# The fifth head pair's keys and queries through the DMA crossbar, more buffers, and a new order of all engines, in a fused attention and gated-convolution kernel

## The chip, the cores and the metric

One core of one Trainium2 chip. The time is device microseconds of one execution of the whole program, as the median of plain runs; one further execution is recorded by the hardware profiler, and all views of the profile are of that one.

## What is computed

Two layers in a row, on a batch of 4 and a sequence of 768. The first is block-sparse attention with 8 heads of 64: blocks of 32 tokens, each of which sees itself and its neighbours, the first and the last block, and three sampled ones.

```python
scores = scale * np.matmul(q, k.transpose(0, 1, 3, 2))        # 4 x 8 x 768 x 768
mask = (np.abs(blk_i - blk_j) <= 1) | (blk_i == 0) | (blk_j == 0) | (blk_i == 23) | (blk_j == 23)
mask |= sampled blocks
attn = softmax(np.where(mask, scores, -1e9))
x = np.matmul(attn, v)                                        # heads side by side: 4 x 768 x 512
h = np.maximum(x @ w_in, 0.0)                                 # 512 -> 1024
conv_out[:, s] = conv_w[0] * h[:, s-1] + conv_w[1] * h[:, s] + conv_w[2] * h[:, s+1]
out = (h * sigmoid(conv_out)) @ w_out                         # 1024 -> 512
```

Inputs and output are float32; the kernel multiplies in bfloat16.

## The kernel before

**Pairs, slots, units.** The 32 heads (4 batches of 8) are taken as 16 pairs P = 0 to 15, four to a batch. A pair's transposed keys and queries lie in two tiles of one of five slots, `e` for even and `o` for odd columns of 128 (64 feature rows, and 24 mask rows below them that add -8000 to forbidden scores). The scores are computed for all 768 keys of a head, half of the queries at a time (a segment: a batch and a half, the last half cut in two, 9 in all). The work is cut into 144 units of 8 blocks of 128 x 128: two groups of score matmuls into a PSUM tile `st` (L746), one exp of 128 x 1024 on ScalarE into `pt` (L757), and two groups of value matmuls into `av` (L779). Pair P of the first batch is first used at unit 4.5 P; pair 4, the fifth, at unit 36, pair 5 at 40.5, pair 6 at 45, pair 7 at 49.5, pair 8 at 72.

**After the attention.** Per segment and pair VectorE normalises `av` into `xtok` (L698), which is transposed to `xT`, for most by a crossbar DMA on SyncE's queue (L707), for a few on TensorE (L717). Then come the first matmul with `winb` into `mix` (L895), ReLU into `hE` (L915 on ScalarE or L917 on VectorE), the convolution as three products and two sums on VectorE (L949, L959; in the last segment as matmuls with diagonal matrices, L970), tanh on ScalarE (L998) and the gate into `gT` (L1001, L1006), the second matmul with `woutb` (L825, the last token tile L810), a copy to `o2s` (L328 on ScalarE, L330 on VectorE; these two lines are the copies of every kind) and the store (L833).

**Keys and queries reach their slots in two ways.** `kq_transposes(P)`, used for P < `NPE` = 5, loads keys (192 KB) and the first query half (96 KB) into `nat`, transposes them on TensorE (6 transposes at L470, 4 at L508) into PSUM and copies them to the slot on VectorE or ScalarE; the second query half goes later through a buffer `nq` (4 more transposes). `kq_crossbar(P)`, used for the rest, loads keys and (up to batch 2) whole queries into `nat`, sends each through the crossbar DMA, keys first, into a staging tile `stg` on SyncE's queue, and then copies both halves on VectorE:

```python
for x, l in ((1, [lk]), (0, lq)):
    xb.append(op("xb", {"SP": 1.4}, lambda e, x=x: nc.sync.dma_start_transpose(          # L585
        out=stg_t[sg.index][:, x].rearrange("p h c s -> p (h c) s"), in_=nat_t[nb.index][:, x]), ...))
for x, t in enumerate((E_t, O_t)):
    def cp(e, x=x, t=t):
        dcopy(e, t[slot.index][0:64], stg_t[sg.index][64 * x:64 * x + 64])                # L330
```

Both copies depend on both crossbars. Loads of keys, queries, values and weights are issued by GpSimd (L240), which also converts to bfloat16. From the second query halves on, they follow the list `SEQ`, and each waits, by a one-element copy on GpSimd (`pace`, L660), until the load four places before it has landed; from the third batch on, a `pace` (L417) reads the result of a set exp instead. The mask rows of slots 3 and 4 are copied by four DMAs on SyncE's queue (L361).

**What sets the order.** There is no run-time scheduler. The operations are collected in a list, and `put_down` issues them in an order written out by hand in the string `ORDER`: two characters name an operation, one more its engine if it may run on several (A is ScalarE, V VectorE, S SyncE), then one for each buffer it takes. Each engine works off its share strictly in that order, and each queue too, so a waiting instruction holds back all behind it on its engine. `NFILL` filler matmuls stand early on TensorE, where it has little else to do.

```python
def put_down(ops, order):
    ...
            o = ops[64 * CODE.index(line[x]) + CODE.index(line[x + 1])]
            if len(engines) > 1:
                e = ENGINES[line[x]]
            for b in o.allocs:
                b.index = CODE.index(line[x])
            ...
                o.fn(e)
```

Of the kernel before, what the change touches and what calls it, by code (L numbers as in the profile page):

```python
# [25 lines left out]
5L5p5q5u0N0J1aV5811bV1S00O0P0Q0R461A0470S481O1490T4a1U14b1V4c2414d2604e274f2c24g2e2591TV34h2f4i2k04j2m34k5H2
5M35v5P05Q5R41pV1oV5z4O15A05U15V5I4PV00I5B25C5J5N5O5W5610625a05S5T5X5Y630661675bV5Z05+5D15EV641656b06c5/060V
6811B11DV1CV6g16h6d26i3ht0hu6l0hq1hrhsV0hvAhO06m6t1hz06u6n46v5hw1hxhAhyAhPhQhBVhRhW16y06z696a6A06D16EhS6F1hT
hF06e1P1hG6fhYhHV6I06j6JhX6k6o6Q16R6q11QV6p06whI06xhJ1RVhZhUh+6r6K26S3hKA6V06WhL16+16/hM6X4705h/0w6s125V4hV0
hC0hDhNVhEVia26B6C6G730747816H6L6M6T1796U6Y1W16Z1Z07507a1i23ib6N21XV46O280296P1/A7g07h7i27l17m717276777n37b7c0  # L30
7q07r7s47j7k7v17w7o7pi0i4i31+Vi51YV7d0i6i1ic7e7x57D07E7t7F07uio07y7z7I17J7N0ii17G17Oijip7Hi77K12g12h7f7A1id7B
i8iei92aV07P27C2bVif7L7S17Tiq7M7Q7R7X07Yik7U37Z42n4l2s14m2u2002v1ig2dV0ih0k2lV1831847Vil88089ir8558a08d18e7W7+
7/0868i08j2iV12tV2imV02jVisV18020K818f18k2iu1iv8q18rix0iyiwA2o02pizViS0iUiT2qV22rViV8s38v08w8x487iD18A18B8C5
iA0iB8F0iE8b8c8G8g8K18h8L2x2w2C2y1822iCAiFA8H02F2G02D28M1i+1iWiXiM0iN8l8S08m2118TiOVi/8U2iP08X18t18Y8u8y8z8D
8Z322Vj0j18n023V8oiQiRA9008E8I8J91iG195196iHiJ0iK8N924975j2iYje3iZj3iIVjf8P1iLV8Qj629d09e8O08V8W8+9i19j9f08/93
9498999n09o9g19hj8j4j79a2j9j5ja9bjhjgji9k19p39s19tjs19x09y9u59z09l9m9qjE09F19r9G9v9K09LjFjb2I2H2Q2N2R22T2O09H2
8p2z2J08R2K9cjjjt9w9A9B09I9J9P19Qjcjdjkjl2AV39M1jujG9R49U09V9N9W3jva019Oa1jHjwA2a50a69Sa25jK19TjL9X9Y2LV42EV3
2MVjIV32BV9C09Da70aa1jN0abjOjMA1a31af0jT1agjUac2jPVk60jVV0Mk8k70Gk9ak1ala4jQ0ah4am32/2S3032Y2Z13231373829E0in
2U0itjJ2Va8jRas0atjSAjW1ax1aya9au1jXjZ0adj+az5jYAj/A2PV4kake19Z19+9/km2knkokpkfkqkbkckhaC0aDaeaiaH1aE0k31aIaj
kgkd1ank4k5Aap2jy0jzaP0aQk01ao0jAavawaAaBaJ2aR4aU1jBaVaZ0k1a+aFkrjCA0aW3a/1aGaKaLjm0b21b3jnb45kik2VaM0ku3aNkj  # L40
kvkwkxb70job8aS0bf1aTaXjpaYkI1bgb90bk0b0b1b5jqA1kkaqklkskyjx33134aOarbh2ktkzkC0kJblkDbm4bp1kKb6bqbabu0bvbb1
2+V02WV02XVkAkBkE35V1bc13a3b13f3cbr3bw1kLkFbibC1bDbH0bIbd39V1kGV336VkMA2kO1kR0kPkSbE5bJ0kTAbM1bNbjbR0bSbnbobs
btkU0bO2bxbykVbW1bXkQVla0lclbbT4kWAbY3bz0ldbAlelfkX1bF0kYc20bGbKbLkZVli1c3c71c8bPl10k+1l2c453d3e3m3p3q03u3n03r
3s3tlglkljl3Vllc91cc0cdce0bQk/ch1cibUl70bVbZcp0b+1l8cqc5l0Vlmcj2lnl41cu1cvcr4cw3c6cal5cz0cAcbcfcgckcE1cFclcB5
cG1be1kHjr3g03hlq2b/2lrlslolhltc0lul9Vcm1l6Vlpcnly3lzlAlBlvlClwlxcs0ctcxcJ0lM0cKlG1cycR1cScClNcDcHcL2cT4cW0cX
cY33E3B3F23J3G3H3C13I3Q3R2lHcIcMcN1c/1d0cUcVcZd40d5lOc+lIlD3v1bBc1cod10d65dc1ddde1cO0lElF3oV2cPlPd2lJdh0di0H
lKV33iV23jVlQA1dj2d3dm1dnm20d7do4m51d8m6dr0m33wd923xV3m4V0m7Adsdw1dxmq0mrdamtms3DV3dt3dy03T3U33Y3V3W3X43440me1
df0dgmh0dkmfmidE0dFdJ1mgAmjAm81dKm9mb0mcdG5maAdL1mu3yVmdVmy1mG2mvmHmAmwmzmBdO0dldpdqdudvdzdPdB1dT1mn1mk0mldA1
dUdHdQ2lRkNlL3K0cQ23L3Z1jD3+dbmmAdV4d/0modImpAlS0e0e13mCmO33MV4mImQdCmJlTe41e5lUlVe60mDmEmKmx0mFlY1lWA13SA4lZ
e90eaeb5l+ee1efdMdNdRdSdWdXe20dY0mPdZe3n00e7ej0e8mLeg1ekl/n1er1m0A2mR45V0mMmS0LmN3/V0el23ldDd+413AmTmUmV3NVec  # L50
edehmW1eiesmXew0exmYn2et4ey3eB1eCeD0mZn3emeG0eHeO1en1ePn4V340Veo2epm+A0nc1nf0ndngeI5eQ1nhAneVnC0nDnEnFnGeT0eU
eueY1evn61eZezeAn7eV2f10f2e+4f33nHn8Vn90eEeFnanbVnu1eJeKf61f7fe0ffeR0eSnl1nmeWnwnveL1nnVnxf80fg5fj1fkfl1eXni0
fo0fpfq2lX3k423O3Peq03ze/njno1ft1f0f4f5fuf9fB0fCnpnInynznkVnJnK2eMnLnr0fa1nsfhfinAfb0nMfcnqVnBnNfv4fD3fG1fHfm
fL0fnfMfrfsfwfxfE0fFntAfI0fy2nOfznS3nTnUnVnWfN5fT1fUfV1o40fJfY0fZn+1o5g11g2fKn/fOfPfW1fXnPf+2g34nXeNm/fdn5fAnQ
nRf/g0g90gag4ge1gfg5gb3o0o6nYnZgg0gj0o7fQ1o8V1g60fRo1gkgr1gsom0ono2A0g7ooV1op1oqgl5orAgc0gdoK0oMgt1os0ghgigw0
gxgmgnotov1owgB1gCgu1go2gpoLoNoOgy2ouAoxAgD4fS1oS1gqg8oH0gK0oIgLoB1oCgvgzgAgEoJAoE0gP1gQgM3oPoFgFgR0oToDVoUoV
# [57 lines left out]
def kernel(  # L114
# [23 lines left out]
    NF, NPE = 4, 5  # L138
# [79 lines left out]
    NFILL = 21  # L218
# [851 lines left out]
```

## Time and profile before

| | |
|---|---|
| plain runs | 206.13 us median of 3 (206.09 to 208.36) |
| the profiled execution | 207.49 us, span on the core 205.7 us |
| TensorE, ScalarE, VectorE, GpSimd busy | 197.3, 190.3, 180.3, 57.9 us |
| DMA moved | 25.96 MB, 126 GB/s on average |
| first and last exp start | 6.72 and 186.60 us |

Busy time of an engine counts the recorded length of each instruction; neighbours overlap in their ends, so an engine at 96% still has some room, and the share says little of a single stage. In the views below a line is given as start, length, engine, line of the code and operation; PE is TensorE, PEld its weight loads, ACT ScalarE, DVE VectorE, POOL GpSimd, SP SyncE, and a q behind the name is the engine's issuing of DMAs. In brackets stands how long the engine was idle ahead of the instruction and what ended it.

### The profile page before, as it was taken

To read this page: it belongs to the slowest core of one execution; us is meant where nothing else is said; L and a number is where in the kernel's file an instruction comes from. 1 tells how busy PE (TensorE), PEld (TensorE's weight loads), DVE (VectorE), ACT (ScalarE), POOL (GpSimd) and SP (SyncE) were. 2 spreads that over 40 slices of the span, in tenths; PEclk is the share of its full clock that TensorE was granted. 3 is DMA by queue.
4 is the path that set the end of the run, shared out by engine and by line. 5 is a ranking of instruction groups with operands and counts; after the bars stand their busy time and mean duration, and the time that the engine had idled before them with its cause. 6 is when DMAs were issued, how large, how long until landed. Compare 5 with 4: busy or idle time off the path is not lost.

```text
span 205.7 us, 6845 instructions
## 1 busy us (share of the span) xinstructions
PE 197.3 (96%) x2698; PEld 154.4 (75%) x2716; DVE 180.3 (88%) x570; ACT 190.3 (93%) x252; POOL 57.9 (28%) x112
## 2 busy tenths in 40 slices
PE   7999999999999999999999999998999999999992
PEld 7789978886688877776788877766688877785761
DVE  6978969997899997999899989979799978999950
ACT  6999999998999999999899999998999999997852
POOL 8870468630514226102415386100000000000000
PEclk9999999999999999999999999999999999999999
DMA  6999999999798983999997999993210401310523
GB/s 147 173 208 208 185 138 117 147 151 189 97 150 96 156 116 35 208 201 192 93 186 88 119 134 225 118 208 72 75 28 3 146 17 29 115 51 17 202 76 133
DMA packets 53655, 25.96 MB, mean 126 GB/s; under 512 B 39616, under 2 KB 50584, under 8 KB 53624
## 3 DMA queue, kind: packets, MB, share of 16 engines
q0 software_dynamic: 19984, 11.24, 45.9%
q1 hardware_dynamic: 33064, 13.60, 34.3%
q10 hardware_dynamic: 576, 0.69, 0.9%
q8 instruction: 21, 0.34, 0.7%
q14 instruction: 10, 0.08, 0.2%
HBM read 23.08 MB, written 6.29 MB: 143 GB/s over the span
## 4 chain that ended last, share of the span: by engine, by line
PE 57%; ACT 16%; DMA 11%; DVE 10%; issue 3%; POOL 0%; ACTq 0%; DVEq 0%
PE st L746 18%; PE mix L895 14%; PE mix L825 13%; ACT pt L757 12%; PE av L779 10%; DMA stg<-nat 6%; DMA nat<-in_k_dram 3%; DVE m L949 3%; DVE m L959 2%; DVE hE L917 2%; DMA o2s<-in_q_dram 1%; PE mix L810 1%; ACT o L328 1%; ACT m L998 1%; DVE xtok L698 1%
## 5 line engine op out<-in xcount | busy, mean ns | idle before, releaser
L757 ACT ACTIVATE pt<-st 128x1024 bf16<-128x1024 f32 x144 | 140.0, 1034 | 2.8 <-PE st L746 2.1
L779 PEld LDWEIGHTS <-pt 128*128 128x128 bf16 x1152 | 51.8, 97 | 9.8
L779 PE MATMUL av<-vt,pt 128*128 128x65 bf16 x1152 | 59.1, 193 | 0.1
L895 PE MATMUL mix<-xT,winb 128*128 128x384 bf16 (+2 forms) x288 | 55.0, 308 | 0.5 <-DVE o2s L330 0.2
L949 DVE TENSOR_SCALAR m<-hE,cw 128x382 bf16<-128x382 bf16 (+2 forms) x192 | 49.0, 314 | 0.6 <-ACT hE L915 0.3
L825 PE MATMUL mix<-woutb,gT 128*128 128x512 bf16 x159 | 43.9, 379 | 1.3 <-DVE gT L1006 0.7
L746 PE MATMUL st<-o 88*128 88x128 bf16 (+1 forms) x240 | 44.4, 229 | 0.2
L746 PE MATMUL st<-o,e 88*128 88x128 bf16 (+1 forms) x228 | 43.4, 233 | 0.4 <-DVE o L330 0.3
L746 PE MATMUL st<-e 88*128 88x128 bf16 (+1 forms) x208 | 41.6, 239 | 0.8 <-ACT pt L757 0.2
L746 PE MATMUL st<-e,o 88*128 88x128 bf16 (+1 forms) x224 | 42.2, 234 | 0.1
L746 PEld LDWEIGHTS <-e 88*128 88x128 bf16 x436 | 33.5, 97 | 10.4 <-issue 1.7
L746 PEld LDWEIGHTS <-o 88*128 88x128 bf16 x464 | 34.9, 97 | 7.8 <-issue 0.9
L959 DVE TENSOR_TENSOR m<-m 128x764 bf16<-128x764 bf16 (+2 forms) x64 | 34.0, 532 | 0.3
L895 PEld LDWEIGHTS <-winb 128*128 128x128 bf16 x288 | 23.2, 97 | 6.6 <-issue 1.1
L998 ACT ACTIVATE m<-m 128x764 bf16<-128x764 bf16 (+2 forms) x32 | 26.4, 826 | 0.2 <-DVE m L959 0.2
L825 PEld LDWEIGHTS <-gT 128*128 128x128 bf16 x184 | 15.7, 97 | 9.6 <-DVE gT L1006 0.8
L417 POOL COPY pace<-pt 1x1 bf16<-1x1 bf16 x24 | 6.4, 267 | 51.3 <-ACT pt L757 51.2
L917 DVE TENSOR_SCALAR hE<-mix 128x384 bf16<-128x384 f32 x28 | 15.4, 554 | 4.0 <-PE mix L895 3.6
L915 ACT ACTIVATE hE<-mix 128x384 bf16<-128x384 f32 (+2 forms) x36 | 17.5, 505 | 1.2 <-PE mix L895 1.0
L1006 DVE TENSOR_TENSOR gT<-m,hE 128x764 bf16<-128x764 bf16 (+3 forms) x36 | 18.1, 510 | 0.4
L698 DVE TENSOR_TENSOR xtok<-av,rcp 128x384 bf16<-128x384 f32 (+2 forms) x36 | 18.1, 506 | 0.4
L240 POOL DMA_DIRECT2D nat<-in_q_dram x23 | 16.8, 733 | 2.7 <-issue 2.5
(84 smaller groups left out, 158.3 us busy)
## 6 DMA issues: line engine op xcount, KB each, us to landing
out_dram<-o2s SPq DMA_DIRECT2D x22, 256.0 KB
vn<-in_v_dram POOLq DMA_DIRECT2D x16, 192.0 KB, 5.5
nat<-in_k_dram POOLq DMA_DIRECT2D x15, 192.0 KB, 4.9
nat<-in_q_dram POOLq DMA_DIRECT2D x7, 192.0 KB, 5.1
winb<-in_moe_w_in_dram POOLq DMA_DIRECT2D x2, 512.0 KB, 9.2
woutb<-in_moe_w_out_dram POOLq DMA_DIRECT2D x4, 256.0 KB, 8.2
nat<-in_q_dram POOLq DMA_DIRECT2D x8, 96.0 KB, 4.6
nq<-in_q_dram POOLq DMA_DIRECT2D x5, 96.0 KB, 5.3
```

The lines of the kernel that those rows point to most:

```text
L698: nm = op("norm", {"DVE": t_dps(128 * C)}, lambda e: nc.vector.tensor_tensor(out=xtok_t[xk.index][:, 0:C].rearrange("p c h d -> p h c d"), ...
L746: nc.tensor.matmul(out=st[:, 128 * x:128 * (x + n_)], lhsT=QK[kc % 2][s][0:88, 1, hh, kc // 2, :], rhs=QK[par][s][0:88, 0, hh, idx:idx + n ...
L757: nc.scalar.activation(out=pt_t[ptb.index], in_=st_t[stb.index], func=AF.Exp, bias=0.0, scale=0.125)
L779: nc.tensor.matmul(out=o[:, off:off + 65], lhsT=pt_t[ptb.index][:, 128 * x:128 * x + 128], rhs=V_t[vslot_b[P].index][:, hh, kc, 0:65], sta ...
L825: nc.tensor.matmul(out=acc(), lhsT=gT_t[gb.index][:, ffc, 128 * t:128 * t + 128], rhs=woutb[:, ffc, :], start=(ffc == 0), stop=(ffc == NFF ...
L895: nc.tensor.matmul(out=mix_t[hb.index][:, w1 * y:w1 * y + w1], lhsT=winb[:, fc, 128 * ffc:128 * ffc + 128], rhs=xT_t[xt_buf[n].index][:, f ...
L915: i = nc.scalar.activation(out=dst, in_=src, func=AF.Relu, bias=0.0, scale=0.5)
L917: i = nc.vector.tensor_scalar(out=dst, in0=src, scalar1=0.5, scalar2=0.0, op0=ALU.mult, op1=ALU.max)
L949: i = nc.vector.tensor_scalar(out=m_t[cb.index][:, x, y, 0:w], in0=hE_t[heb.index][:, f0 + y, t0 + x:t0 + x + w], scalar1=cw[:, x, f0 + y: ...
L959: nc.vector.tensor_tensor(out=m[:, a_, :, 0:w], in0=m[:, a_, :, 0:w], in1=m[:, b_, :, 0:w], op=ALU.add)
L998: th = [op("tanh", {"ACT": t_act(2 * w) + 0.04}, lambda e, cb=cb, w=w: nc.scalar.activation(out=m_t[cb.index][:, 0, :, 0:w], in_=m_t[cb.in ...
L1006: i = nc.vector.tensor_tensor(out=gT_t[gtb.index][:, f0:f0 + 2, t0:t1], in0=m_t[cb.index][:, 0, :, 0:w], in1=hE_t[heb.index][:, f0:f0 + 2, ...
```

## The change

`NPE` falls from 5 to 4, so pair 4 is made by `kq_crossbar` instead of `kq_transposes`; its second query load (`nq4`) leaves `SEQ`, and its first becomes a load of both halves. Eight kinds of buffer get one or two more: staging tiles 2 to 3, `nat` 4 to 5, value loads `vn` 3 to 4, `pt` 6 to 8, `xtok` 3 to 4, `xT` 3 to 4, the gate's `m` 4 to 5, output `o2s` 4 to 5. Two filler matmuls go. `ORDER` is another string throughout; the operations are the same but for pair 4.

```diff
 ORDER = """
-000b1e0010x020y030407080a0905060c0e0gV0d0WV10hA0UA0oA0f0B0z0i0XV0mV0VV0lV0nV0t0v1f1c01q11s21t1801E21G31m11Hr41
...
+0a0407080905060y000b1e01f1c01q11s11t1E21G21801m10102030A1H1S30O0P0Q0R0c0e0gV0d0WV30UV0hA0oA0f0x0iqZ1q+q/r0r1r2
...
-    NF, NPE = 4, 5
+    NF, NPE = 4, 4
     WHOLE = ()
-    SEQ = "nq0 nq1 w0 w1 nq2 w2 nq3 w3 k4 q4 v4 k5 q5 v5 k6 q6 v6 k7 q7 v7 nq4"
+    SEQ = "nq0 nq1 w0 w1 nq2 w2 nq3 w3 k4 q4 v4 k5 q5 v5 k6 q6 v6 k7 q7 v7"
...
-    NSLOT, NSTG, NNAT, NVN, NPT, NXK, NXT, NHE, NCV, NGT, NOS = 5, 2, 4, 3, 6, 3, 3, 2, 4, 2, 4
+    NSLOT, NSTG, NNAT, NVN, NPT, NXK, NXT, NHE, NCV, NGT, NOS = 5, 3, 5, 4, 8, 4, 4, 2, 5, 2, 5
...
-    NFILL = 21
+    NFILL = 19
```

In the new order the engines' instructions differ so. ScalarE: 3 of the 28 ReLUs of 128 x 384 and one value copy go to VectorE, one output copy comes from there, and the head's small copies are dealt anew. TensorE: 14 transposes and 2 fillers fewer. SyncE's queue begins, after the first loads and the two mask copies of slot 3, with the crossbars of pair 4, the two mask copies of slot 4 and the crossbars of pair 5; the first feature transpose follows them, then pair 6, three feature transposes and pair 7. Before, the feature transpose came first, and they alternated. GpSimd's queue has the same loads in nearly the same order, without `nq4`.

More of the change, by code (lines that the diff above doesn't have):

```diff
@@ L26 @@
[L26 to L55, printed above, removed]
@@ new lines @@
+bjaVaWbf434313233513936kdaGkpkok61kqkekv1krksa+kB0kCaHakklkm2QV0kt2RV2/V1kua/bk1kwbn0bokxb3bv1bwbp6kDb40kykE
+bx3bA0bB2UV0b50kFV0b630VkzA3bF1bC5kK1bGkH0kIbH7kLbbbK0bLbP1kMAkJVl32l4l5l6l7bM0kQ0bcbQkN1kRkObgbhbX0bYbR2kSA
+c01blbmkPAlb4bZ4c1bqc21kW0kXbrc50by1bzbDc6bEca1cbl8lcld33V1bs2kYVbtlel9lfkT1bIbJbNkUbOc73373j3k2383g3h03o3l3m
+3n3vcc6lgkVVbSci0cjbT0bU1lab+kZ0ck5bVlj3cn1col01l1k+cp7lllhk/Vl2Acs0b/c3ctc4c8c9cx1cdcecylF1lklmcf3lr0lilnlslt
+cglulvcu0cz2cC0cDcE4cl1cmcqcrcK1cLcM1lojk3a1b70bukG3p0bW3b3qchlz0lAcP0cvcwcQcR3lGcU1cVcAcBcFcG0cNcOcScTcZ0c+lp
@@ L62 @@
+qYAqIqJqKqLA1qMA
 """
```

44 lines of the change are left out of this document (34 added, 10 removed).

## The prediction

> **What bounds the kernel now.** I read the busy shares first, then busy time by stage, then the timelines of ScalarE, VectorE and the two issuing queues around pairs 4 and 5, where the change is made.
>
> ```profile
> PE 197.3 (96%) x2698; PEld 154.4 (75%) x2716; DVE 180.3 (88%) x570; ACT 190.3 (93%) x252; POOL 57.9 (28%) x112
> ```
>
> Three engines are near full, so the span is close to work divided among them, and a wait costs only where all three run out of cover. The stages show where that is:
>
> ```profile
> core 0: us, PE busy (x) PEld busy (x) DVE busy (x) ACT busy (x) POOL busy (x), PEclk, DMA share, GB/s
> 6.70:20.00 13.30, 12.90 (x216) 11.60 (x217) 10.95 (x34) 13.18 (x17) 6.79 (x10) 1.00 1.29 201
> 31.00:44.00 13.00, 12.67 (x219) 10.81 (x217) 12.89 (x40) 12.93 (x17) 9.29 (x18) 1.00 1.12 141
> 44.00:60.00 16.00, 15.13 (x191) 11.23 (x193) 13.82 (x40) 14.96 (x19) 2.73 (x6) 1.00 1.37 149
> 60.00:75.00 15.00, 14.82 (x237) 12.11 (x237) 14.79 (x45) 15.00 (x18) 5.30 (x10) 1.00 0.92 121
> 187.60:205.70 18.10, 14.00 (x121) 8.90 (x121) 10.50 (x44) 9.50 (x23) 0.00 (x0) 0.99 0.32 117
> ```
>
> From 6.7 to 20 us ScalarE alone is full (13.18 of 13.30) while VectorE has 2.4 us free. From 31 to 44 VectorE and ScalarE are both full. From 44 to 60 none is: TensorE 0.9 short, ScalarE 1.0, VectorE 2.2, with the DMA share at its highest. The last 18 us are a chain with 4 us of TensorE idle. The clock is full nearly throughout, so it plays no part. The timelines say what was missing at 44 to 60 (first ScalarE, then VectorE):
>
> ```profile
> 10.66 17.72 ACT L757 ACTIVATE pt<-st 128x1024 bf16<-128x1024 f32 x19
> 50.61 4.76 ACT L757 ACTIVATE pt<-st 128x1024 bf16<-128x1024 f32 x5 [0.65 <-PE st L746]
> ```
>
> ```profile
> 49.05 0.55 DVE L330 COPY e<-stg 64x1536 bf16<-64x1536 bf16 x1 [1.21 <-DMA stg<-nat]
> 52.91 0.55 DVE L330 COPY e<-stg 64x1536 bf16<-64x1536 bf16 x1 [0.71 <-DMA stg<-nat]
> ```
>
> The copies out of the staging tile wait for the crossbar of pairs 5 and 6, and exp 40, the first of pair 5, starts 0.65 us late behind that. The third such wait (1.1 us, near 75) is on VectorE alone. Sync's queue and GpSimd's show why it landed late:
>
> ```profile
> 36.59 1.30 SPq L707 DMA_TRANSPOSE xT<-xtok  x1
> 37.99 3.15 SPq L585 DMA_TRANSPOSE stg<-nat  x2
> ```
>
> ```profile
> 26.57 0.72 POOL L240 DMA_DIRECT2D nat<-in_k_dram  x1
> 27.61 0.72 POOL L240 DMA_DIRECT2D nat<-in_q_dram  x1
> 31.07 0.72 POOL L240 DMA_DIRECT2D nat<-in_k_dram  x1 [0.20 <-issue]
> 32.09 0.76 POOL L240 DMA_DIRECT2D nat<-in_q_dram  x1
> ```
>
> Pair 5's loads are issued at 31.07 and 32.09, but its two crossbars only at 37.99 to 41.14: the feature transpose at 36.59 stands ahead of them in Sync's queue and waits for VectorE's normalisation. The data then take 49.05 - 41.14 = 7.9 us.
>
> **The change, part by part.** Durations are rows of this execution, which took 207.49 us: the 205.74 us span and 1.75 around it. The median of the plain runs is 206.13, so I work out a difference and take it from the median.
>
> ```profile
> L330 DVE COPY e<-stg 64x1536 bf16<-64x1536 bf16 x11 | 5.9, 548 | 3.0 <-DMA stg<-nat 3.0
> L470 PE MATMUL mix<-ident,nat 128*128 128x128 bf16 x27 | 2.3, 219 | 0.0
> q0 software_dynamic: 19984, 11.24, 45.9%
> q1 hardware_dynamic: 33064, 13.60, 34.3%
> ```
>
> *Pair 4 to the crossbar.* TensorE loses 6 key and 8 query transposes. Ten ran from 39.35 to 40.19 and four took 0.39 us at 61.34: 1.23 us at most; at the spacing inside those groups, (0.50 - 0.22) / 5 = 0.056, 14 are 0.78. VectorE loses copies of 0.50, 0.56, 0.41, 0.41 and 0.30 = 2.18 and gains two staging copies, 0.55 + 0.58 = 1.13; ScalarE loses one of 0.37. The bytes loaded stay the same (one query load of 192 KB for two of 96). New are two crossbars of 0.197 MB. The page gives that queue 34.3% of 205.7 us for 13.60 MB, 5.2 us of all 16 engines per MB, so 1.0 us each, 2.0 us in a stretch whose DMA share is 1.1 to 1.4.
>
> *When they land.* Key and query loads issue at 26.6 and 27.6 and take the page's median 4.9 and 5.1: there at 31.5 and 32.7. Sync's queue is empty then (in the new order these two stand ahead of the feature transposes, after only two mask copies); at 1.25 us an issue the second goes out by 34. With 5.0 us (the transpose at 132.04 on the chain of waits) to 7.9 us after that, they land between 39 and 42. In the new order the first staging copy stands between two old places on VectorE that fell at 40.0 and 43.0; by its work ahead, at about 41.5, or 40.7 with ScalarE's lead below. So from 1.7 early to 1.3 late: nearest to the row under the same load, 7.9, which is 1 late. I price this at 0.4 and keep -0 and +1.3. Queued behind that copy on VectorE are the normalisations and convolutions, hence the next feature transposes.
>
> *Pairs 5 and 6.* Their crossbars no longer stand behind the feature transpose at 36.59 and can issue when their loads are there, about 37 to 39: 2 us earlier. The third staging buffer lets pair 6 follow without waiting for pair 5's copies. That removes up to 1.21 + 0.71 of VectorE's waits and the 0.65 + 0.33 of ScalarE's. Behind it stand two crossbars more on the DMA engines, 2.0 us. I take 0.6 off, bounds 0 and 1.9. The mask copies for slot 4, moved behind pair 4's crossbars, are 1.5 us of issue with 7 us to spare; they cost nothing unless pair 4 itself is late.
>
> A rule of the Trainium skill speaks against both items: "DMA: Bandwidth & Descriptors", section "Queues, rings and completion order", says that each DMA engine takes turns, packet by packet, between the queue rows with work. By it pair 4's crossbars take turns with the software loads of pairs 5 to 7 and delay them, instead of filling gaps, and both items would become losses; the slow rival below is what that gives. The 7.9 us of pair 5, issued among loads, agrees with it.
>
> *Buffers.* The fourth value buffer removes a 1.32 us wait of GpSimd at 11.0 for VectorE; nothing on the chain waits for that load. The fifth output buffer and the others lift limits that no wait above shows: nothing, bounds 0 and 0.3. One memset more at the start and two filler matmuls fewer lie in idle time.
>
> *The new order.* Between ScalarE and VectorE work changes hands: three ReLUs (507 ns on ScalarE, 554 on VectorE) and one value copy (853, 366) go to VectorE, one output copy (587, 685) comes back, and a few head copies are dealt anew. By rows with the overlap of neighbours out (exp 0.925 from the 19 in 17.72 us, tanh 0.74, ReLU 0.38, output copy 0.47) I added the work that stands ahead of chosen exps on ScalarE, and likewise on TensorE and VectorE, in both orders. The new one has on ScalarE 0.9 us less ahead of exp 24, 0.7 at exp 48, 1.1 at 60, 3.0 at 72, 2.6 at 108, 1.8 at 143 and at the end. TensorE: 0.7, 1.2, 2.4, 2.8, 2.5, 1.5, and 0.9 less at the end. VectorE: 1.7 less at 24, but 1.1 more at 48, 2.0 less at 60, 1.6 less at 143, 0.3 more at the end. So the lead of 0.9 that ScalarE wins in its own stage is spent on VectorE before exp 48, and what counts at the end is TensorE's total: 0.9 off, bounds 0 (VectorE's +0.3 decides) and 3.0 (the largest lead is kept).
>
> *Tail.* After exp 143 TensorE has 0.6 more left than before (that is in the 0.9), the chain of the last segment is the same.
>
> *Sum.* -0.9 (work) - 0.6 (waits of pairs 5 and 6) + 0.4 (pair 4 late) - 0.4 (of the lead through the first stage, what the 2.2 us that VectorE has free at 44 to 60 lets through) = -1.5. That is 206.0 for the profiled execution and **204.6** for the median.
>
> **The rivals.**
>
> *The crossbars come late (slower).* One mechanism: the two added crossbars and pair 4's loads share the DMA engines with the loads and crossbars of pairs 5 to 7. For it: share 1.37 at 44 to 60 and 7.9 us after issue. Against: they now start 6 us sooner, when Sync's queue carried nothing. It decides once pair 4's second crossbar lands later than 9 us after issue, at 43, since exp 36 needs it at 44.7 less the two copies. Price: the waits stay (+0.6 to the sum), pair 4 late by 1.3 instead of 0.4 (+0.9) and pair 5 by the 2.0 us of added service: -1.5 + 3.5 = +2.0, 208.1; with pair 6 pushed by another 2.0, 210.1, and with pair 7 as well past the 2%.
>
> *VectorE eats it (no change).* Its total is 0.3 higher and it is full at 31 to 44 and 60 to 75. Then the lead is 0, and only the waits move: -0.6 + 0.4 + 0.3 = 206.2. For: VectorE's 1.1 more ahead of exp 48. Against: it has 2.4 us free before 20 and 7.6 at the end.
>
> *The whole lead is kept (faster).* The 3.0 us of exp 72 hold through the end as waits of the later stages fall too, with 1.9 of waits gone at pairs 5 and 6 and pair 4 on time: 3.0 + 1.9 = 4.9, less the 0.6 in the tail: 4.3, 201.8. Against: ScalarE's lead shrinks to 1.8 by exp 143 by its own order.
>
> **How the numbers follow.** The forecast has 0.48 (203.4 to 205.6), no change 0.18, late crossbars 0.17, the whole lead 0.17. Two per cent, about what a measurement of this kernel can tell from no change, is 202.0 and 210.3. Over half of the last case lies below 202.0 (0.13 with a little of the forecast's edge); of the slow case half lies past 210.3, with all the pairs late (0.08). That leaves 0.79 within. The range leaves out the far halves of both: 201.9 to 208.6.
>
> **What would show it.** Right: the first staging copy starts before 42 with under 1 us of waiting; VectorE's waits for staging fall from 3.0 to under 1.5; exp 24 starts about 0.8 earlier than 31.25, exp 72 by 1.5 to 3 earlier than 88.8; the last exp at 185. Wrong in sign: exp 36 later than 44.7 with a ScalarE wait behind a staging copy, or the DMA share of 31 to 44 near 1.4 and loads at 7 us. Wrong in size: the last exp before 183, or the tail not 18.1 but shorter by over 1.

## The result, and the profile after

| kernel | median | runs | ratio to the kernel before, same chip |
|---|---|---|---|
| before | 207.91 us (206.09 to 208.92) | 6 | 1 |
| after | 215.71 us (214.57 to 218.01) | 6 | 1.0386, 95% interval 1.0318 to 1.0454 |

The change makes the kernel slower by 3.9%; forecast was 204.6 us in a range of 201.9 to 208.6. Some runs of a kernel take over 1.5% longer than its fastest, most of them with TensorE a little below full clock; the ratios in this text leave such runs out, and the medians hold all runs. The experiments ran on several chips, so their times are compared by the ratio to the kernel before on the same chip.

The page of the profiled execution after (215.80 us, span 214.0):

```profile
span 214.0 us, 6794 instructions
PE 199.8 (93%) x2682; PEld 155.3 (73%) x2700; DVE 181.5 (85%) x573; ACT 188.5 (88%) x246; POOL 58.7 (27%) x110
PE   7899999975389999999999999999999999999992
ACT  6999999985338999999989999999999998997851
PEclk9999999998858999999999999999999999999999
L757 ACT ACTIVATE pt<-st 128x1024 bf16<-128x1024 f32 x144 | 141.4, 1036 | 11.1 <-PE st L746 10.3
```

The rows of TensorE and ScalarE have one dent, at slices 9 to 12 of 5.35 us, and the clock has one a slice later. ScalarE stands 11.1 us ahead of the exps, 10.3 of it for score matmuls; before it was 2.8, with 2.1 for them:

```profile
L757 ACT ACTIVATE pt<-st 128x1024 bf16<-128x1024 f32 x144 | 140.0, 1034 | 2.8 <-PE st L746 2.1
```

Busy time by stage after the change, same stages as before:

```profile
core 0: us, PE busy (x) PEld busy (x) DVE busy (x) ACT busy (x) POOL busy (x), PEclk, DMA share, GB/s
6.70:20.00 13.30, 12.82 (x224) 11.65 (x223) 12.14 (x35) 13.22 (x16) 6.57 (x10) 1.00 1.31 202
31.00:44.00 13.00, 12.53 (x212) 10.39 (x210) 11.40 (x34) 12.66 (x17) 6.25 (x13) 1.00 1.48 150
44.00:60.00 16.00, 9.07 (x99) 6.08 (x98) 8.17 (x24) 8.50 (x9) 3.13 (x7) 0.85 1.63 136
60.00:75.00 15.00, 15.00 (x157) 11.09 (x155) 12.28 (x38) 11.96 (x15) 3.72 (x7) 0.82 0.53 82
```

From 44 to 60 all three engines stand for almost half of the time, with the DMA share at 1.63 (1.37 before). Starts of chosen exps, from the timelines of ScalarE, put the loss between two of them:

| exp | 24 | 36 | 40 | 44 | 48 | 72 | 108 | 143 |
|---|---|---|---|---|---|---|---|---|
| before | 31.25 | 44.72 | 50.61 | 54.34 | 59.80 | 88.82 | 134.71 | 186.60 |
| after | 30.20 | 43.98 | 52.44 | 63.95 | 69.16 | 96.57 | 142.42 | 194.79 |
| difference | -1.05 | -0.74 | +1.83 | +9.61 | +9.36 | +7.75 | +7.71 | +8.19 |

The first stage gains what was forecast. Everything is lost between exp 36 and exp 44; after that the distance stays between 7.7 and 9.6 us. What stood there is on VectorE's timeline, the first staging copies of pairs 4, 5 and 6:

```profile
42.21 0.55 DVE L330 COPY e<-stg 64x1536 bf16<-64x1536 bf16 x1 [1.48 <-DMA stg<-nat]
50.05 0.55 DVE L330 COPY e<-stg 64x1536 bf16<-64x1536 bf16 x1 [2.47 <-DMA stg<-nat]
57.78 0.55 DVE L330 COPY e<-stg 64x1536 bf16<-64x1536 bf16 x1 [5.27 <-DMA stg<-nat]
```

Before, pair 5's came at 49.05 and pair 6's at 52.91. Pair 4 is almost on time, pair 5 is 1.0 late, pair 6 is 4.9 late. The chain of waits (start, duration, what) tells how pair 6 came to 57.78 and what hung on it:

```profile
34.98 10.61 DMA nat<-in_q_dram
...
45.64 12.12 DMA stg<-nat
...
57.78 0.55 DVE e L330
...
58.87 0.48 DVE gT L1006
...
59.40 1.04 PE mix L825 x2
60.43 0.85 PE st L746 x6
```

Pair 6's second crossbar is issued at 45.64, when its query load is there; before, it was issued at 45.56. So it starts no later. But it took 12.12 us, and before, by the same view, 7.25:

```profile
45.56 7.25 DMA stg<-nat
```

The 4.87 us between them are the whole lateness of pair 6 (57.78 less 52.91). What was in flight beside it is the later loads. In the stretch of 30 to 56 us the software loads have these medians from issue to landing, after the change and then before it:

```profile
nat<-in_k_dram POOLq DMA_DIRECT2D x4, 192.0 KB, 8.1
nat<-in_q_dram POOLq DMA_DIRECT2D x3, 192.0 KB, 10.6
vn<-in_v_dram POOLq DMA_DIRECT2D x3, 192.0 KB, 10.3
```

```profile
nat<-in_k_dram POOLq DMA_DIRECT2D x4, 192.0 KB, 5.2
nat<-in_q_dram POOLq DMA_DIRECT2D x4, 192.0 KB, 5.1
vn<-in_v_dram POOLq DMA_DIRECT2D x3, 192.0 KB, 5.5
```

In these 26 us the DMA engines moved no more than before, 3.60 MB against 3.65; what rose is their packet time, a share of 1.63 against 1.27. A load is held back until the load four places ahead of it has landed, so late loads make later ones: pair 7's keys, query and values are issued at 41.44, 43.39 and 46.16 instead of 39.01, 39.96 and 41.95, right into the time of pair 6's crossbars.

Behind the staging copy in VectorE's queue stood the product gT, and behind the output matmul that waits for gT (L825) stood, in TensorE's queue, the score matmuls that ScalarE waits for. One late transfer stops three engines:

```profile
59.40 1.04 PE L825 MATMUL mix<-woutb,gT 128*128 128x512 bf16 x2 [3.77 <-DVE gT L1006]
```

```profile
61.38 1.02 ACT L757 ACTIVATE pt<-st 128x1024 bf16<-128x1024 f32 x1 [4.76 <-PE st L746]
```

### The profile page after: what moved, and what is told of

The parts are those of the page before. It is cut to its first block, busy times and chain, and to the rows that moved or that the text cites. A ratio compares the mean times of both kernels' runs of the same rounds, so it can differ in the third digit from the quotient of the medians.

```text
span 214.0 us, 6794 instructions
## 1 busy us (share of the span) xinstructions
PE 199.8 (93%) x2682; PEld 155.3 (73%) x2700; DVE 181.5 (85%) x573; ACT 188.5 (88%) x246; POOL 58.7 (27%) x110
## 4 chain that ended last, share of the span: by engine, by line
PE 64%; DMA 17%; DVE 8%; ACT 5%; issue 3%; POOL 1%; SPq 0%; POOLq 0%; ACTq 0%; DVEq 0%
PE st L746 20%; PE mix L895 14%; PE mix L825 14%; PE av L779 10%; DMA stg<-nat 8%; DMA nat<-in_q_dram 5%; ACT pt L757 3%; DMA nat<-in_k_dram 2%; DMA woutb<-in_moe_w_out_dram 2%; PE st L1027 1%; DVE m L949 1%; PE mix L810 1%; DVE e L330 1%; DVE o L330 1%; DVE hE L917 1%
## 5 line engine op out<-in xcount | busy, mean ns | idle before, releaser
L757 ACT ACTIVATE pt<-st 128x1024 bf16<-128x1024 f32 x144 | 141.4, 1036 | 11.1 <-PE st L746 10.3
L779 PE MATMUL av<-vt,pt 128*128 128x65 bf16 x1152 | 57.9, 193 | 1.1 <-DVE vt L330 0.7
L779 PEld LDWEIGHTS <-pt 128*128 128x128 bf16 x1152 | 51.0, 97 | 10.8 <-issue 1.5
L825 PE MATMUL mix<-woutb,gT 128*128 128x512 bf16 x159 | 45.2, 390 | 4.4 <-DVE gT L1006 3.8
L746 PE MATMUL st<-o,e 88*128 88x128 bf16 (+1 forms) x228 | 44.8, 236 | 1.3 <-DVE o L330 1.3
L746 PE MATMUL st<-e 88*128 88x128 bf16 (+1 forms) x208 | 42.5, 245 | 1.4 <-DVE e L330 1.1
L895 PEld LDWEIGHTS <-winb 128*128 128x128 bf16 x288 | 24.1, 98 | 7.6 <-issue 0.8
L825 PEld LDWEIGHTS <-gT 128*128 128x128 bf16 x184 | 15.7, 99 | 12.7 <-DVE gT L1006 4.1
L417 POOL COPY pace<-pt 1x1 bf16<-1x1 bf16 x24 | 8.4, 349 | 56.8 <-ACT pt L757 55.2
L917 DVE TENSOR_SCALAR hE<-mix 128x384 bf16<-128x384 f32 x31 | 17.0, 552 | 3.0 <-PE mix L895 2.6
L915 ACT ACTIVATE hE<-mix 128x384 bf16<-128x384 f32 (+2 forms) x33 | 16.2, 508 | 1.0 <-PE mix L895 0.8
```

The source lines that it names most:

```text
L746: nc.tensor.matmul(out=st[:, 128 * x:128 * (x + n_)], lhsT=QK[kc % 2][s][0:88, 1, hh, kc // 2, :], rhs=QK[par][s][0:88, 0, hh, idx:idx + n ...
L757: nc.scalar.activation(out=pt_t[ptb.index], in_=st_t[stb.index], func=AF.Exp, bias=0.0, scale=0.125)
L779: nc.tensor.matmul(out=o[:, off:off + 65], lhsT=pt_t[ptb.index][:, 128 * x:128 * x + 128], rhs=V_t[vslot_b[P].index][:, hh, kc, 0:65], sta ...
L825: nc.tensor.matmul(out=acc(), lhsT=gT_t[gb.index][:, ffc, 128 * t:128 * t + 128], rhs=woutb[:, ffc, :], start=(ffc == 0), stop=(ffc == NFF ...
L895: nc.tensor.matmul(out=mix_t[hb.index][:, w1 * y:w1 * y + w1], lhsT=winb[:, fc, 128 * ffc:128 * ffc + 128], rhs=xT_t[xt_buf[n].index][:, f ...
L917: i = nc.vector.tensor_scalar(out=dst, in0=src, scalar1=0.5, scalar2=0.0, op0=ALU.mult, op1=ALU.max)
```

## The experiments

Five theories, by the letters that the expectations use. A: crossbars and software loads slow each other by more than their own service. B: the mask copies of slot 4, now behind pair 4's crossbars, come too late. C: the new order itself is bad. D: no such harm, but the DMA engines are full from 25 to 60 us, every added transfer pushes what stands behind it by its own service, and the new order puts more ahead of pair 6. E: a part of the loss is TensorE at half clock after it has stood. Pair numbers in the diffs are those of the text; "xb" is a crossbar of keys or queries, "x_xb" one of normalised features.

**One part at a time: the buffers.**

```diff
 # kernel before
-NSLOT, ... NOS = 5, 2, 4, 3, 6, 3, 3, 2, 4, 2, 4
+NSLOT, ... NOS = 5, 3, 5, 4, 8, 4, 4, 2, 5, 2, 5
```

> The kernel before with the new numbers of buffers alone; the order is the old one, so it never takes the new ones. Theory A (crossbars among loads): no difference, 206 to 208 us, ratio 1.00 to 0.3%. Rival B (mask copies between the crossbars) and rival C (the new order of Sync's queue): the same. Only a rival by which the memory layout itself costs something says more than 1%.

207.95 us, ratio 1.0027 (0.9983 to 1.0071). More buffers alone do nothing.

**Pair 4 by the crossbar, in the old order.**

```diff
 # kernel before
-NF, NPE = 4, 5
+NF, NPE = 4, 4
 # Sync's queue
+xb k4, xb q4
 x_xb 0, xb k5, xb q5, x_xb 1, xb k6, ...
```

> The kernel before with one part of the change alone: pair 4 by the crossbar, its two crossbars put ahead of the first feature transpose on Sync's queue and its staging copies where the key copies stood; the four mask copies stay early, two staging tiles, old order otherwise. Theory A, that crossbars and the software loads of pairs 5 to 7 hold each other up when both are in flight, says slower by 3 to 9 us with loads of 8 us and more near 35 and staging waits over 5 us. Rival B, that the mask copies of slot 4 between the crossbars are what jams the queue, says within 1.5 us of before. Rival C, that the new order of Sync's queue and the third staging tile do it, says within 2 us of before.

209.42 us, ratio 1.0008 (0.9939 to 1.0078), where A had put down 3 to 9 us. The 10 runs spread from 205.1 to 212.05 and the ratio rests on four of them, so no exact price can be read from it. But it shows no loss: the harm is not shown for the two crossbars alone, only for the crossbars together with the new order.

**The mask copies ahead of the crossbars.**

```diff
 # kernel after, Sync's queue
-xb k4, xb q4, mask e, mask o, xb k5, ...
+mask e, mask o, xb k4, xb q4, xb k5, ...
```

> The changed kernel with the two mask copies of slot 4 put back ahead of pair 4's crossbars, right behind those of slot 3. Theory A: gains at most 2 us of the 8, the 12 us crossbar of pair 6 stays over 8. Rival B: gains 5 to 9 us, near 207 to 209, and the loads at 35 land in about 5 us. Rival C: no gain.

215.46 us, ratio 1.04 (1.0308 to 1.0493): no gain in time, so B falls as the main cause. In the profiled execution (213.54 us) pairs 5 and 6 are copied at 46.67 and 55.78, 3.4 and 2.0 us sooner than in the changed kernel; a small part of the lateness may be the mask copies'.

**Pair 4 back on TensorE, in the new order.**

```diff
 # kernel after
-NF, NPE = 4, 4
+NF, NPE = 4, 5
 # in the order, by hand: transposes and copies of pair 4 beside exp 36
```

> The changed kernel with pair 4 back on TensorE's transposes (its second query load again on GpSimd's queue), all else of the new order and the buffers kept; the mask copies then stand ahead of pair 5's crossbars. Theory A: gains 4 to 9 us, 207 to 211. Rival B: gains little, under 2, as the mask copies still stand in Sync's queue. Rival C: gains little, under 2, with staging waits of over 6 us at 44 to 60.

211.11 us, ratio 1.0201 (1.0107 to 1.0295): about half of the loss, 1.9 of 3.9 points, goes with the two crossbars, and pair 6's first copy comes at 52.15 instead of 57.78. But ScalarE waits 2.56 us at 44.76 for one of the copies put back, so what the order is worth by itself isn't in this number; four more attempts follow below.

**The transfers by themselves.** Six loads of 128 x 768 by GpSimd's queue, six crossbars of the same size by Sync's, alone and together, with nothing else in the kernel.

```diff
+for i in range(6): nc.gpsimd.dma_start(soft[i], pair)           # alone
+for i in range(6): nc.sync.dma_start_transpose(stg[i], src[i])  # alone
+for i in range(6): both                                         # together
```

> No attention and no layer: only DMAs, six phases one after the other, each begun when the one before has landed. Six software loads of 192 KB (GpSimd's queue, float32 to bfloat16); six crossbars of 128 x 768 (Sync's queue); both together; six plain float32 loads of ScalarE's queue; these and six crossbars; software loads and crossbars again, the crossbars first. The output is not computed. Theory A (crossbars and software loads in flight together hold each other up beyond their own service): the phases with both take over 1.3 times the sum of the two alone. Rival D (only the sum of the service, the engines are simply full): both together take 1.0 to 1.1 times the sum, or less. If plain loads mix freely and software loads do not, the fifth phase is at or under its sum and the third and sixth are over.

The first three stretches of one execution, each from its first issue to the last landing, by the windows view:

```profile
core 0: us, DVE busy (x) POOL busy (x), PEclk, DMA share, GB/s
3.69:13.37 9.68, 0.71 (x6) 4.39 (x6) 1.00 0.87 122
13.94:23.47 9.53, 2.81 (x23) 0.00 (x0) 1.00 0.68 125
24.00:41.37 17.37, 3.34 (x30) 4.29 (x6) 1.00 1.07 136
```

and the issues with their median time to landing (alone, and beside the crossbars):

```profile
soft<-in_q_dram POOLq DMA_DIRECT2D x6, 192.0 KB, 5.2
soft<-in_k_dram POOLq DMA_DIRECT2D x6, 192.0 KB, 8.7
```

Together they take 17.37 us where the two alone add up to 19.21, although the loads start only 2.4 us after the first crossbar (26.38 and 24.0). It is not worse than one after the other, so A falls here as it was put, with over 1.3 times the sum. But hardly anything is hidden: a crossbar beside loads adds (17.37 - 9.68) / 6 = 1.28 us, and a load lands in 8.7 us instead of 5.2. Alone, the DMA engines had time to spare in both stretches; by their shares the packets take 0.87 x 9.68 + 0.68 x 9.53 = 14.9 us, and together 1.07 x 17.37 = 18.6. So each packet does take longer in company, by a quarter on the mean. D comes nearest here, with a little of A in it. The other three stretches say the same: the mix once more, with the crossbars first, takes 17.57 us; six plain float32 loads on ScalarE's queue take 10.4 us alone and, with six crossbars, 18.8, which is 0.94 of the sum. So it is not a matter of software loads only.

**Fewer loads in flight.**

```diff
 # kernel after: each load waits on GpSimd for the load
-    d, buf, src = seq[x - 4]
+    d, buf, src = seq[x - 2]
```

> The changed kernel with one number changed: each load on GpSimd's list waits for the load two places before it, not four, so that at most two software loads are in flight beside the crossbars. Theory A: pair 4's second crossbar and pair 6's land sooner (under 8 us after issue instead of 12), gain of 2 to 6 us, 210 to 214. Rival D: the same bytes by the same engines, and the loads only start later: no gain, 215 to 219.

218.66 us, ratio 1.0594 (1.0521 to 1.0666), pair 6's first copy at 60.33. With fewer loads in flight each lands sooner (medians of 4.1 to 5.2 us from 30 to 56 us, for 8.1 to 10.6), but it starts later, and pair 6 comes later. The time is what D had put down; A's shorter landings came as well, and did not pay.

**Loads of pairs 6 and 7 held for pair 4.**

```diff
 # kernel after, GpSimd's queue
+wait until xb q4 has landed
 k6 q6 v6 k7 q7 v7
```

> The changed kernel with the loads of pairs 6 and 7 (keys, queries and values) held back until pair 4's second crossbar has landed: the wait ahead of pair 6's key load reads the staging tile instead of an earlier load. Theory A: pair 4's and 5's crossbars land in 5 us, the held loads in 5 us as well, and as nothing is in each other's way pair 6 comes sooner than 57.8 although its load starts later: gain of 2 to 7 us, 209 to 214. Rival D: pair 6 comes as late as its load is held, 4 to 6 us later: 217 to 221.

214.85 us, 210.85 to 215.41 in 4 runs, too wide for a ratio: no gain is shown in time. But D, which had put down 217 to 221 us and pair 6 late by 4 to 6 us more, is wrong here: no run took that long. In the profiled execution (215.1 us) pair 6's key load starts at 42.17 instead of 32.83, and its copy still comes sooner, 55.31 for 57.78; pair 5's comes at 47.58 for 50.05. In one execution that is a hint at A: transfers that run together hold each other up by more than their own service.

**The clock.** 106 matmuls that nothing reads, in the places where TensorE stood.

```diff
 # kernel after
+106 filler matmuls between exp 36 and exp 48
```

> The changed kernel with 106 filler matmuls on TensorE (128 x 128, a free part of the score PSUM), 40 in the score group of unit 40 where TensorE waits for pair 5's staging copies and 66 ahead of the matmul that waits 3.8 us at 59.4; no wait is taken away. Theory E, that a part of the loss is TensorE at half clock after these waits (51.7 to 55.1 and 58.5 to 65.3 us in the records): granted clock 0.99 or more, gain of 2 to 4 us, 212 to 214. If the half clock costs nothing because the copies are late anyway, within 1 us of 215.5.

213.75 us, ratio 1.0342 (1.0225 to 1.0458); TensorE's clock stays full there, and pair 6's copy still comes at 57.55. The median is 2.0 us below that of the changed kernel, the lower edge of E's forecast; by the ratios it is 0.4 of 3.9 points, and the intervals overlap. So the half clock is worth some 2 us by these medians, perhaps less, and most of the loss is not the clock.

**Two crossbars that nothing reads, in the kernel before.**

```diff
 # kernel before, pair 4 still by transposes; Sync's queue
+xb k4 -> spare tile, twice
 x_xb 0, xb k5, xb q5, ...
```

> The kernel before, with pair 4 still transposed by TensorE and everything else in its old place; added are two crossbars of pair 4's keys into a third staging tile that nothing reads, issued ahead of the first feature transpose. They cost nothing but DMA service and 2.5 us of Sync's queue. Theory D: pair 5's and pair 6's loads and crossbars land 2.6 us later together (1.3 each), pair 6's first staging copy comes at 54 to 56 instead of 52.9, and the time is 2 to 4 us above the kernel before. Rival (DMA service is cheap, what costs in the change is what waits for pair 4's own copies): within 0.5 us of the kernel before.

210.41 us, 206.0 to 212.16 in 4 runs, too wide for a ratio. It decides nothing between D and its rival.

**Pair 5's crossbars first, in the kernel before.**

```diff
 # kernel before, Sync's queue
-x_xb 0, xb k5, xb q5, x_xb 1, ...
+xb k5, xb q5, x_xb 0, x_xb 1, ...
```

> The kernel before with one move: pair 5's two crossbars stand ahead of the first feature transpose in Sync's queue. The prediction's term for pairs 5 and 6 taken alone: issue at about 35 instead of 38.0, staging copy 1 to 2 us sooner than 49.05, so 0.5 to 1 us faster than before if nothing else pays. Theory D: what pair 5's crossbars gain the loads of pairs 6 and 7 lose, since the DMA engines are busy throughout: pair 6's copies no earlier than 52.9 and the time the same within 0.5 us.

205.90 us, ratio 0.9935 (0.9887 to 0.9983): a little faster than both kernels, by one move in a queue. The copies of pairs 5 and 6:

```profile
48.72 0.54 DVE L330 COPY e<-stg 64x1536 bf16<-64x1536 bf16 x1
51.77 0.54 DVE L330 COPY e<-stg 64x1536 bf16<-64x1536 bf16 x1
```

```profile
31.00:44.00 13.00, 12.74 (x220) 10.88 (x218) 12.89 (x40) 12.93 (x18) 8.41 (x17) 1.00 1.30 156
44.00:60.00 16.00, 15.57 (x202) 11.87 (x204) 14.92 (x44) 15.75 (x21) 3.77 (x7) 1.00 1.15 148
```

Neither waits any more, and pair 6 gains 1.14 where D had expected nothing. From 44 to 60 TensorE is busy for 15.57 us (15.13 before), ScalarE for 15.75 (14.96). D's forecast for this run was wrong: a transfer issued sooner used DMA time that had been free, the share of 31 to 44 goes from 1.12 to 1.30 while that of 44 to 60 falls from 1.37 to 1.15. The DMA engines of the kernel before are not full throughout; there was room at 31 to 38, where the share goes from 1.04 to 1.23.

**The loads in another order, everything of the change kept.**

```diff
 # kernel after, GpSimd's queue
-SEQ = "... k4 q4 v4 k5 q5 v5 k6 q6 v6 k7 q7 v7"
+SEQ = "... k4 q4 k5 q5 k6 q6 v4 v5 k7 q7 v6 v7"
```

> The changed kernel with one reordering: the software loads of pairs 4 to 7 come as k4 q4 k5 q5 k6 q6 v4 v5 k7 q7 v6 v7, so pair 6's keys and queries start two places sooner and the values of pairs 4 and 5 behind them. Theory D: these two loads are worth 1.2 us each of full DMA engines, so pair 6's crossbars land about 2.5 us sooner (copies near 55 instead of 57.8) and the time falls by 1 to 4 us, as long as pair 4's value copy (45.8) does not become late; then it takes back a part. Rival C (the new order is bad, not the data): 215 to 216 as before.

213.90 us, ratio 1.0322 (1.0235 to 1.0409); pair 6's copy at 55.94, 1.84 sooner. The median is 1.8 us lower; by the ratios it is 0.6 points, with intervals that overlap, so the copy moved as D had it and a gain in time is not clear of noise. (A load by itself took 9.68 / 6 = 1.6 us above, not the 1.2 put down here.)

**... and pair 7's loads held until pair 5 is there.**

```diff
 # kernel after, GpSimd's queue
-SEQ = "... k4 q4 v4 k5 q5 v5 k6 q6 v6 k7 q7 v7"
+SEQ = "... k4 q4 k5 q5 k6 q6 v4 v5 v6 v7 k7 q7"
+# before k7: wait until xb q5 has landed
```

> The changed kernel, everything of it kept, with the software loads in the order k4 q4 k5 q5 k6 q6 v4 v5 v6 v7 k7 q7 and the last two held on GpSimd's queue until pair 5's second crossbar has landed. It takes two loads out of the time in which pair 6's crossbars are under way, beside what e12 did. Theory D (what is late is late by the sum of the transfers ahead of it): pair 6's copies 2 to 3 us sooner than e12's 55.94, near 53 to 54, and the time 210 to 212. Rival (pair 6's crossbars are slow in themselves, or something other than DMA service holds them): copies near 56, time near the 213.9 of e12.

210.89 us, ratio 1.0119 (1.0034 to 1.0204). Copies of pairs 4, 5 and 6, and the busy time from 44 to 60:

```profile
40.80 0.66 DVE L330 COPY e<-stg 64x1536 bf16<-64x1536 bf16 x1
48.05 0.55 DVE L330 COPY e<-stg 64x1536 bf16<-64x1536 bf16 x1 [1.76 <-DMA stg<-nat]
51.76 0.55 DVE L330 COPY e<-stg 64x1536 bf16<-64x1536 bf16 x1 [1.25 <-DMA stg<-nat]
```

```profile
44.00:60.00 16.00, 12.61 (x141) 8.82 (x141) 11.11 (x32) 12.70 (x15) 5.39 (x9) 1.00 1.39 174
```

The same transfers, the same crossbars, the same work, the same order on the other engines: only which load goes when is changed. Pair 7's keys and query go out at 49.32 and 50.50 instead of 41.44 and 43.39. Pair 6 comes 6.02 us sooner (57.78 to 51.76), the clock stays full, and the loss falls from 3.9% to 1.2%. This is the run that shows the cause: what was late was late by the loads that ran beside it. It is more than D had asked for (53 to 54), and the windows say that service isn't a constant either: from 44 to 60 the DMA engines moved 174 GB/s at a share of 1.39, and in the changed kernel 136 GB/s at 1.63, though not quite the same transfers fall into the stretch. From 30 to 56 it is 3.92 MB at 1.43 against 3.60 at 1.63: more bytes in less packet time. So D's plain sum of service is too simple, here as with the loads held for pair 4, and in the kernel there is more of A than in the transfers by themselves. What in the mix of loads and crossbars makes packets longer was not tried further. What is left is 1.2%; TensorE still stands 3.4 us from 44 to 60.

**The theory applied to the kernel before.**

```diff
 # kernel before, Sync's queue as in the move of pair 5's crossbars, and
-SEQ = "... k5 q5 v5 k6 q6 v6 k7 q7 v7 nq4"
+SEQ = "... k5 q5 k6 q6 v5 k7 q7 v6 v7 nq4"
```

> The kernel before with two moves and no added transfer: pair 5's crossbars ahead of the first feature transpose (as e11) and pair 6's key and query loads one place sooner, ahead of pair 5's values. Theory D: one load of 1.2 us less ahead of pair 6, so its first copy at 50.5 to 51.5 (51.77 in e11, 52.91 before) and the time 0 to 0.7 us below e11's ratio of 0.9935, that is 0.990 to 0.994 of the kernel before. Rival (e11 already has all there is, the three engines are full from 44 to 60): 0.993 to 0.996.

205.67 us, ratio 0.9949 (0.9907 to 0.9991): faster than before again, but no better than the single move, as the rival had it, and pair 6's copy at 52.31 missed the 50.5 to 51.5. Sync's queue gives a reason:

```profile
35.92 2.65 SPq L585 DMA_TRANSPOSE stg<-nat  x2
38.67 3.36 SPq L707 DMA_TRANSPOSE xT<-xtok  x2
42.12 4.63 SPq L585 DMA_TRANSPOSE stg<-nat  x2
```

Pair 6's query load is issued 2.5 us sooner than with the single move (33.75 against 36.23), but its crossbars still stand behind the second feature transpose and go out at 42.12 (42.59): the early load waits in a queue.

**The new order without the crossbar, four more times.** Each puts pair 4's transposes in another place, to be rid of the stall that the one before had.

```diff
 # kernel after, NF, NPE = 4, 5; transposes and copies of pair 4:
+transposes ahead of exp 33                         # first
+keys before score matmul 60, query after exp 31    # second
+as second, last query copy on VectorE              # third
+as first, query copies two multiplications later   # fourth
```

> The changed kernel's order and buffers, with pair 4's keys and queries by TensorE transposes again, this time placed before exp 33 instead of beside exp 36 (in e4 ScalarE waited 2.6 us there). Theory D (the two added crossbars fill DMA engines that are already full, and the rest of the order is sound): with two crossbars fewer pair 6's staging copies come at about 53 to 54 instead of 57.8, exp 36 at 44 to 45, exp 48 near 60 and the whole at 206 to 209, that is 211.1 of e4 less its 2.6 us. Rival C (the new order itself is bad, whatever moves the data): 210 to 212 as e4 had, with the loss of some 4 us still between exp 36 and 48.

> The changed kernel's order and buffers with pair 4 by TensorE transposes once more; the key transposes now stand before score matmul 60 and the query's after exp 31, so that no copy of pair 4 stands in VectorE's queue before its transpose has run (in e4b one stood 2.1 us). It gives the new order by itself. The prediction's term (the new order leads by 0.9 and keeps some of it): 206 to 207.5, below the kernel before of the same chip by 0.5 to 1.5. Rival C (the new order is at best equal, its first-stage lead is spent before exp 48): equal to the kernel before within 0.5 us or above it.

> The new order with pair 4 by transposes as in e13, but the query's second copy on VectorE instead of ScalarE and the feed-forward matmuls back where the new order has them: in e13 TensorE waited 2.30 us at 42.65 for that ScalarE copy, and VectorE 2.51 behind it. If the new order is good (the prediction's term), exp 36 is at 44.5 to 45.5 and the time 206.5 to 208, at or below the kernel before of the same chip. Rival C (the order itself is late before exp 48): exp 48 still at 60.5 or later and the time 209 to 210.

> The new order with pair 4 by transposes as in e4b, with both query copies two multiplications later on VectorE's queue (in e4b VectorE stood 2.12 us at 42.43 for the query's transposes). Same two readings as for e16: 206.5 to 208 if the order is good, 209 to 210 if it is late by itself. If e16 and e17 differ by over 1 us, it is still the place of the copies that decides and the order by itself stays open.

| | median | ratio | exp 36 | exp 48 | exp 143 |
|---|---|---|---|---|---|
| first | 209.44 | 1.0113 (1.0072 to 1.0155) | 46.94 | 60.63 | 187.88 |
| second | 210.03 | 1.0108 (1.0031 to 1.0186) | 47.46 | 61.14 | 189.15 |
| third | 208.42 | 1.0124 (1.0074 to 1.0174) | 46.29 | 61.08 | 188.05 |
| fourth | 209.81 | 1.0201 (1.0134 to 1.0267) | 46.45 | 61.60 | 188.89 |

None is as fast as the kernel before. But in all four, and in the first try above, pair 6's first copy comes at 52.1 to 53.1 (52.91 before): its lateness goes with pair 4's crossbars. What these runs still lose is something else. The third has only short waits left on ScalarE and VectorE from 31 to 52 us (in all, times, longest):

```profile
ACT m L998 <- DVE m L959: 0.7, 1, 0.7
ACT pt L757 <- PE st L746: 0.7, 1, 0.7
DVE m L949 <- ACT hE L915: 0.5, 1, 0.5
```

The two of ScalarE, at 38.41 and 40.12, make up 1.35 of the 1.57 us by which exp 36 is late; and in this run exp 24 comes at 31.26, so there is no lead of the first stage to lose. The third and the fourth differ by 1.4 us, which by the expectation leaves the order by itself open: the place of the copies decides. Whether the order would be good with pair 4 by a crossbar that costs no DMA time can't be told: it was not possible to have the one without the other. That the order by itself is worth -0.9 us is not borne out by any run. That it is bad by itself (C) is not shown either, but every run of it lies at least 1.1% above the kernel before, the one with pair 7's loads held among them, so C may be what is left.

## Why the prediction was wrong, point by point

**What bounds the kernel.** Right: three engines near full, and the stretch of 44 to 60 with the DMA share at its highest is where the time was decided. The prediction read that share as a price on single transfers and not as a queue.

**Pair 4 to the crossbar, and when it lands.** Right in time, in part by luck. The copy was put at 41.5, and 0.4 late; it came at 42.21 after 1.48 us of waiting on VectorE, a little over the 42 and the 1 us that were to show it right. The second crossbar's issue ended at 32.82 (30.09 and 2.73), 1.2 sooner than the 34 put down, and the copy came 9.4 us after that, where 5.0 to 7.9 were allowed: a first sign of slow transfers, hidden by the early start. ScalarE waited 0.32 for exp 36, which started at 43.98, still 0.74 sooner than before:

```profile
30.09 2.73 SPq L585 DMA_TRANSPOSE stg<-nat  x2
```

```profile
43.98 1.02 ACT L757 ACTIVATE pt<-st 128x1024 bf16<-128x1024 f32 x1 [0.32 <-PE st L746]
```

**The price of a crossbar.** Mis-sized: 1.0 us from the page's average of its queue, 1.28 measured beside loads, 2.6 instead of 2.0 for two. The average is one over the whole span, in company and alone; the price was wanted for the stretch with the most company.

**Pairs 5 and 6: -0.6 with bounds of 0 and -1.9.** This is the step that failed, and in sign. Its first half held: pair 5's crossbars were issued at 34.53 and 38.01, the first earlier than the 37 to 39 put down. But it took "issued 2 us earlier" for "there 2 us earlier", and weighed the two new crossbars against pair 5 alone. Pair 4's crossbars and pair 5's now ran among the loads, whose median went from 5 to between 8 and 10.6 us; the pacing passed that on to pair 7's loads, and these ran beside pair 6's crossbars, which took 12.12 us for 7.25. The term measures +1.0 for pair 5 and +4.9 for pair 6, and VectorE's waits for staging tiles rose from 3.0 to 9.6 us instead of falling below 1.5. Its lower bound, no gain, did not reach below nothing, although the text itself put 2.0 us of DMA service behind it.

**What pair 6 then cost.** Left out: the queues behind the late copy. With 1.83 us lost by exp 40 and pair 6 late by 4.9, exp 44 was 9.6 late, because VectorE, TensorE and ScalarE each stood behind the copy, and because TensorE came back at half clock. That the clock plays no part was true of the kernel before only; its share is the 2 us or less of the filler run, and no run splits the rest.

**The mask copies and the buffers at nothing.** Right in time, by the two runs that take them one by one, to within their intervals of 0.4 and 0.9%.

**The new order.** Its first step was right: 0.9 less ahead of exp 24 forecast, 1.05 measured. In the other profiled executions of the new order exp 24 comes between 29.89 and 31.26 (31.25 before), so the lead is there in most and its size is no more certain than that. The -0.9 at the end is not seen in any run; the further -0.4 of the sum, for what is left of the first lead, is worked out from nothing but the 2.2 us that VectorE has free, and no run shows it. The way it was counted, work ahead of an exp on each engine, says when the engines could be there and nothing of the data.

**The tail.** Right: from exp 143 to the end 19.1 us before and 19.2 after.

**The rivals.** The slow one named the mechanism that happened, crossbars sharing the DMA engines with the loads and crossbars of pairs 5 to 7, and the signs put down for it came: the DMA share of 31 to 44 was 1.48, and loads took over 7 us. Two things in it were wrong. It was to decide once pair 4's second crossbar landed after 43; that landed in time for a copy at 42.21, and the harm came all the same, two pairs later. And its price was +2.0, 4.0 with pair 6, where the last exp came 8.2 later: service was counted once, without the later loads that the pacing pushes on, and without the engines behind the copy. The rule that "DMA: Bandwidth & Descriptors" of the Trainium skill gives in "Queues, rings and completion order", that a DMA engine takes turns packet by packet between the rows with work, agrees with the transfers by themselves: with both queues busy, loads and crossbars end together near the end of the sum (17.37 of 19.21 us), instead of one filling the gaps of the other. With it the slow case deserved more than 0.17.

## What to carry to other kernels

Treat the DMA engines as one server with a list of due times: for each staged tile add up every transfer that will be in flight with its own, loads and transposes alike and those issued after it too, and look at the tiles that are due later, not only at the one that is added. The sum is a first guide only: with pair 5's crossbars first, and with pair 7's loads held, pair 6 came sooner than it said. When data is late, first change which transfer goes first: one move in a queue was worth 0.65% on the kernel before, and another order of loads alone brought the loss from 3.9% to 1.2% here. And a wait is priced by what stands behind it in each engine's queue, so a copy that may be late does not belong in front of work that another engine needs.

## What the runs showed of the hardware

Crossbars by themselves: six of 128 x 768 take 9.53 us at a DMA share of 0.68, so for them it seems to be the issue, about 1.3 us each, that sets the pace. Six software loads take 9.68 us at 0.87; the two kinds together hardly overlap, 17.37 us, with packets a quarter longer. In the kernel the DMA engines moved 136 or 174 GB/s from 44 to 60 us, by the order of the loads.

Once, the half clock came after less idleness than expected. By "TensorE: Matmul & The Clock Gate" of the Trainium skill, section "Why this matters for your kernels", it is gaps of over about 3 us between bursts that bring it. The second drop here agrees nearly: TensorE stood for 3.77 us before 59.40, and the mean clock of 0.63 from 58 to 60 puts the drop at about 58.5, after 2.9 us of it. The first does not: the mean of 0.92 from 50 to 52 puts it at about 51.7, in the second of two waits of 1.08 and 1.03 us with one matmul between them.

```profile
50.66 0.28 PE L746 MATMUL st<-e 88*128 88x256 bf16 x1 [1.08 <-DVE e L330]
51.97 0.27 PE L746 MATMUL st<-o,e 88*128 88x128 bf16 x1 [1.03 <-DVE o L330]
```

```profile
50.00:52.00 2.00, 0.31 (x2) 0.92 1.65 161
52.00:54.00 2.00, 2.00 (x10) 0.50 1.90 143
56.00:58.00 2.00, 0.00 (x0) 1.00 0.87 131
58.00:60.00 2.00, 0.60 (x2) 0.63 1.33 226
60.00:62.00 2.00, 2.00 (x11) 0.50 1.39 200
```

The columns are TensorE's busy time, its instructions, the clock, the DMA share and GB/s. In the run with pair 7's loads held, waits of 1.03 and 1.23 us that lay 3.4 us apart left the clock at 1.00. So one long gap is not needed for the half clock; which measure of idle time counts, these runs do not show.
